# Scaling seven float64 weight pieces on GpSimd, with a new order table, in an attention and expert kernel

## The chip, the cores and the metric

The kernel runs on one core of a Trainium2 chip. The metric is the device time of one execution in microseconds (us); lower is better. The core's engines each follow a queue of their own: TensorE (PE; its weight loads are listed apart as PEld), VectorE (DVE), ScalarE (ACT), GpSimd (POOL) and SyncE (SP), which issues nearly all transfers.

## The reference

Three stages follow one another on 4 batches of 576 tokens: Nyström attention with 32 landmarks and a six-step inverse, a gated layer with 512 inputs and 1536 hidden columns, and eight routed experts.

```python
A = sm(q, k_lm);  Bm = sm(q_lm, k_lm);  C = sm(q_lm, k)
Z = Bm.transpose(0, 1, 3, 2) / (norm1(Bm) * norminf(Bm) + 1e-06)
for _ in range(6):
    Z = 2 * Z - Z @ Bm @ Z
x = A @ Z @ C @ v

xn = x / np.sqrt(np.mean(x * x, axis=-1, keepdims=True) + 1e-06) * rms_g
g = xn @ w_gate
x = (g * (1.0 / (1.0 + np.exp(-g))) * (xn @ w_val)) @ w_out

# routed experts: tokens with x @ w_skip > 0 pick the expert e of the largest logit
out = x + gate_w * (np.maximum(x @ w1[e], 0.0) @ w2[e])   # other tokens: out = x
```

The change concerns w_gate and w_val, each 512x1536. They reach the kernel, as w_out does, as **float64**, while the engines compute in 32 bits.

## The kernel before, in words

**Stages.** `attention()` computes one batch; the first batch's attention takes the first 55 us or so. The gated layer then runs as eight units (`run_unit`, lines 1302 to 1336), each of half a batch (288 tokens). A unit goes over 12 columns of 128 hidden features: products pg (gate) and pv (value), the activation in `hidden_g` and `hidden_v`, and the result split into a high and a low 32-bit-rounded part, h_t. Then the "o" products with w_out follow. The later batches' attention runs beside the first units. The routed experts (products ph and py) come last.

**Attention is multiplied into the weights.** The layer's input is attention's A (normalised, ap, split into ap_t) times a small matrix WT per head pair; so the kernel first multiplies WT into the weights, P = WT x w, and splits P into two parts (a ScalarE cast and a VectorE subtraction). For one batch P is made in column groups q = 0 to 2 (tiles P_678, P_682, P_1001). The factor 1/rms reaches ap by way of sq, ms, a square root on ScalarE (rbs), a reciprocal on VectorE, the rb products and the copies of rb to rbs.

**From float64 to 32 bits.** w_gate and w_val come in 12 pieces (`PARTS`, line 917; for each q two of w_gate and two of w_val), each one load of 1 MB into one of three raw buffers (`load_raw`, tiles wr). `from_f64` (lines 826 to 846) makes a piece in four steps:

1. *scaling*: the upper word of each number, read as a 32-bit float, times a power of two, into a tile s (two buffers);
2. a conversion on ScalarE of the top 16 bits to integers (wo<-wr, int32<-uint16);
3. a conversion on ScalarE that writes the half word (wo<-wr, f16<-f32);
4. *joining* on VectorE: shift s by three bits and OR it in (SCALAR_TENSOR_TENSOR wo<-s,wo).

`convert_w(i)` (line 870) calls it with the engines `EARLY` for pieces 0 to 4 and `LATE` for 5 to 11 (the seven later pieces). The load of piece i+3 needs the raw buffer of piece i, so steps 1 to 3 of piece i must be over. The finished piece is also written to a spill in memory (wg_d, wv_d), from which later batches read it. `convert_wout` does the same for the 12 pieces of w_out (wf<-wo, x<-wo on ScalarE, then a split, whose subtraction alternates between VectorE and GpSimd).

**The order.** `ORDER` (lines 38 and on) holds for TensorE, VectorE, ScalarE, GpSimd and SyncE a list of signed numbers, pairs of a jump and a run length. `arrange()` walks each list and chains the engine's instructions in the order that it gives. So each engine's order is written out by hand, instruction by instruction. An engine executes its queue in that order, and a step that waits holds all that stand behind it.

Line numbers are those of the kernel before (those of after are larger by 13). Most of the profile's rows carry L175 or L198, the lines of the helper through which all instructions are recorded, so tile names tell the rows apart.

Of the kernel before, what the change touches and what calls it, by code (L numbers as in the profile page):

```python
# [11 lines left out]
ALU = mybir.AluOpType  # L12
# [19 lines left out]
F64_BIAS = 2.0**-112  # L32
# [7 lines left out]
    for s in (  # L40
# [162 lines left out]
def attention_moe_kernel(  # L203
# [644 lines left out]
    EARLY, LATE, WOUT = (V, A, A), (V, A, A), (V, A, A)  # L848
# [689 lines left out]
```

## Time and profile before

| | |
|---|---|
| median of three runs | 656.9 us (655.61 to 657.79) |
| profiled execution | 652.86 us |
| its span, first to last instruction | 651.1 us |
| mean granted TensorE clock | 0.975 |
| TensorE busy | 615.8 us, 95% |
| VectorE busy | 435.4 us, 67% |
| ScalarE busy | 271.0 us, 42% |
| GpSimd busy | 142.6 us, 22% |

All views come from one profiled execution. The granted clock is a share of full speed: 1.00 is 2.4 GHz and 0.50 is 1.2 GHz. Busy times of single stages tell more than those of the span, as the stages have different limits.

### The profile page before, as it was taken

Reading aid. Unit: us, or ns where it says so; the run is one execution under the profiler, and the core shown is the slowest. Engines: PE = TensorE matmul, PEld = TensorE weight load, DVE = VectorE, ACT = ScalarE, POOL = GpSimd, SP = SyncE. Lnnn points to the kernel's source line nnn. Section 1 sums busy time; section 2 is a strip of 40 time slices with the busy share of each in tenths; the row PEclk is TensorE's granted clock in tenths of the full one; section 3 lists DMA queues with packets and bytes.
Section 4 is the critical chain, followed back from the end, with each engine's and each line's share of the span. In section 5 each row is a group of like instructions: output and inputs, shape, how many; then the busy total and the mean of one; then the engine's idle time right before and its main releaser. Section 6 shows DMA issues by size and latency. Waiting matters only on the chain.

```text
span 651.1 us, 12738 instructions
## 1 busy us (share of the span) xinstructions
PE 615.8 (95%) x4712; PEld 536.8 (82%) x4712; DVE 435.4 (67%) x1013; ACT 271.0 (42%) x583; POOL 142.6 (22%) x162
## 2 busy tenths in 40 slices
PE   5878689999989999999999999999999999999996
PEld 5755469888858889779988878999998989989985
DVE  8888878989778788879589773723626344354361
ACT  2676779342155224435323443412533434333240
POOL 5000234322004104201401310321632133033030
PEclk9868789999999999999999999999999999999999
DMA  9887990541365222169122043302175476183363
GB/s 293 286 259 272 373 403 5 174 118 49 90 227 199 59 91 74 36 231 266 42 74 56 2 146 111 114 2 81 56 205 154 147 232 190 47 256 105 111 210 122
DMA packets 68685, 97.13 MB, mean 149 GB/s; under 512 B 11152, under 2 KB 46224, under 8 KB 68624
## 3 DMA queue, kind: packets, MB, share of 16 engines
q1 hardware_dynamic: 68624, 96.33, 46.1%
q8 instruction: 37, 0.61, 0.4%
q14 instruction: 24, 0.20, 0.1%
HBM read 76.97 MB, written 19.34 MB: 148 GB/s over the span
## 4 chain that ended last, share of the span: by engine, by line
PE 58%; DMA 2%; DVE 1%; POOL 1%; ACT 1%; issue 0%; ACTq 0%; DVEq 0%; POOLq 0%
PE o L175 12%; PE py L175 12%; PE ph L175 12%; PE pv L175 8%; PE pg L175 7%; PE P L175 2%; PE sq L175 1%; DMA w1r<-in_moe_w_dram 1%; PE nr L175 1%; PE lp L175 1%; DMA w2r<-in_moe_w_dram 1%; PE sk L175 1%; POOL xsl L175 1%; PE cT L175 0%; PE rb L175 0%
## 5 line engine op out<-in xcount | busy, mean ns | idle before, releaser
L175 PE MATMUL o<-h_t,wo 128*128 128x288 f32 x1152 | 164.0, 298 | 0.8 <-DVE wo L175 0.7
L175 PEld LDWEIGHTS o<-h_t,wo 128*128 128x128 f32 x1152 | 154.5, 188 | 10.4 <-issue 8.1
L175 POOL TENSOR_TENSOR h_t<-h,h_t 128x288 fp32r<-128x288 f32 x96 | 80.8, 845 | 323.7 <-ACT h_t L175 279.1
L175 PE MATMUL pv<-ap_t,P 128*128 128x288 f32 x576 | 100.7, 308 | 6.4 <-ACT P L175 4.4
L175 PE MATMUL pg<-ap_t,P 128*128 128x288 f32 x576 | 100.1, 307 | 4.5 <-ACT P L175 2.4
L175 PEld LDWEIGHTS pg<-ap_t,P 128*128 128x128 f32 x576 | 85.1, 194 | 13.0 <-ACT P L175 5.1
L175 PEld LDWEIGHTS pv<-ap_t,P 128*128 128x128 f32 x576 | 85.3, 195 | 11.5 <-ACT P L175 7.4
L175 PE MATMUL ph<-xsh,P 128*128 128x288 f32 x384 | 77.6, 297 | 0.0
L175 ACT ACTIVATE h<-pg 128x288 f32<-128x288 f32 x96 | 39.4, 411 | 66.9 <-PE pg L175 63.3
L175 PEld LDWEIGHTS ph<-xsh,P 128*128 128x128 f32 x384 | 61.7, 188 | 0.6
L175 DVE SCALAR_TENSOR_TENSOR h<-h,pg 128x288 f32<-128x288 f32 x96 | 43.0, 448 | 27.3 <-ACT h L175 27.2
L175 PE MATMUL ph<-xsl,P 128*128 128x288 f32 x192 | 55.5, 296 | 0.0
L175 PE MATMUL py<-wo,h_t 128*128 128x512 f32 x210 | 52.2, 395 | 0.0
L175 ACT CAST h_t<-h 128x288 fp32r<-128x288 f32 x96 | 40.8, 430 | 24.6 <-DVE h L175 24.3
L175 DVE TENSOR_TENSOR h<-h,pv 128x288 f32<-128x288 f32 x96 | 43.0, 451 | 9.6 <-PE pv L175 3.3
L175 PEld LDWEIGHTS py<-wo,h_t 128*128 128x128 f32 x210 | 39.3, 188 | 9.5
L175 POOL TENSOR_TENSOR P<-w1r,P 128x512 fp32r<-128x512 f32 x16 | 21.0, 1311 | 83.6 <-ACT P L175 81.5
L175 DVE STREAM_TRANSPOSE T<-kq 64x576 f32<-64x576 f32 (+1 forms) x40 | 35.6, 891 | 5.2 <-DMA kq<-in_q_dram 4.2
L175 DVE SCALAR_TENSOR_TENSOR h_t<-ph,h_t 128x288 fp32r<-128x288 f32 (+2 forms) x45 | 14.5, 353 | 32.4 <-ACT h_t L175 32.4
L175 PEld LDWEIGHTS ph<-xsl,P 128*128 128x128 f32 x192 | 35.7, 188 | 0.2
L175 DVE TENSOR_TENSOR P<-P,P 128x512 fp32r<-128x512 f32 x48 | 31.2, 682 | 4.9 <-ACT P L175 4.7
L175 ACT CAST P<-w1r 128x512 fp32r<-128x512 f32 x32 | 19.9, 621 | 32.5 <-DMA w1r<-in_moe_w_dram 31.6
(215 smaller groups left out, 830.0 us busy)
## 6 DMA issues: line engine op xcount, KB each, us to landing
wl<-wg_d SPq DMA_DIRECT2D x18, 512.0 KB, 5.1
wr<-wv_d SPq DMA_DIRECT2D x16, 512.0 KB, 4.8
w1r<-in_moe_w_dram SPq DMA_DIRECT2D x32, 256.0 KB, 3.1
wr<-in_moe_w_gate_dram SPq DMA_DIRECT2D x6, 1024.0 KB, 8.4
wr<-in_moe_w_val_dram SPq DMA_DIRECT2D x6, 1024.0 KB, 6.2
wo<-in_moe_w_out_dram SPq DMA_DIRECT2D x12, 512.0 KB, 10.0
wo<-in_moe_w_dram SPq DMA_DIRECT2D x24, 256.0 KB, 5.2
kq<-in_k_dram SPq DMA_DIRECT2D x8, 576.0 KB, 4.6
```

Of the source, the lines that this page charges most:

```text
L175: ins = f(*args, **kw)
```

## The change

`from_f64` lets its scaling run on the engine that it is given, not always on VectorE, and `LATE` names GpSimd for it. All five lists of `ORDER` are new. Every instruction other than the seven scalings stays on its engine.

```diff
@@ the table: all five lists are replaced; the first line of the first list @@
-        "0 9 2 9 -11 2 9 5 3 4 -7 3 4 5 2 17 -18 1 -2 1 18 9 1 1 -2 1 5 1 -4 1 -2 1 1 2 1 "
+        "0 9 2 9 -11 2 9 16 3 17 -20 2 25 3 -28 1 17 7 3 2 3 1 -4 3 1 1 1 1 -2 1 1 5 5 1 "
...
@@ -832,7 +845,7 @@
         if on[0] is A:
             A.activation(s, hi, AF.Copy, scale=F64_BIAS)
         else:
-            V.tensor_scalar(s, hi, F64_BIAS, None, ALU.mult)
+            on[0].tensor_scalar(s, hi, F64_BIAS, None, ALU.mult)
         if on[1] is A:
             A.activation(di, top, AF.Copy, scale=LOW_BITS)
         else:
@@ -845,7 +858,7 @@
             di, si, 3, di, ALU.logical_shift_left, ALU.bitwise_or
         )
 
-    EARLY, LATE, WOUT = (V, A, A), (V, A, A), (V, A, A)
+    EARLY, LATE, WOUT = (V, A, A), (G, A, A), (V, A, A)
     wsrc = {"g": w_gate, "v": w_val}
     wparts = {}
 
```

In the rows below, wr is a raw piece, s_822 to s_988 are the scaled tiles of the seven later pieces, and wo the converted piece. GpSimd, from the end of the landmark sums (ln) on, before:

```order
L175 TENSOR_TENSOR ln<-s_340 128x64
L175 TENSOR_TENSOR h_t<-h,h_t 128x288 x7
L175 TENSOR_TENSOR wo<-wf,wo 128x512
L175 TENSOR_TENSOR h_t<-h,h_t 128x288 x2
L175 TENSOR_TENSOR wo<-x_1184,wo 128x512
```

and after:

```order
L188 TENSOR_TENSOR ln<-s_340 128x64
L188 TENSOR_SCALAR s_822<-wr 128x1024
L188 TENSOR_SCALAR s_831<-wr 128x1024
L188 TENSOR_SCALAR s_840<-wr 128x1024
L188 TENSOR_SCALAR s_883<-wr 128x1024
L188 TENSOR_SCALAR s_942<-wr 128x1024
L188 TENSOR_SCALAR s_981<-wr 128x1024
L188 TENSOR_TENSOR h_t<-h,h_t 128x288
L188 TENSOR_SCALAR s_988<-wr 128x1024
L188 TENSOR_TENSOR h_t<-h,h_t 128x288 x3
L188 TENSOR_TENSOR wo<-wf,wo 128x512
```

Six scalings stand ahead of the first h_t of the layer and one behind it.

VectorE, from the squares (sq) of the first batch's attention to the first h, before:

```order
L175 TENSOR_TENSOR sq<-sq 128x576
L175 TENSOR_SCALAR s_822<-wr 128x1024
L175 TENSOR_SCALAR rbs<-ms 128x144
L175 TENSOR_TENSOR WT<-pw,gcol 128x256
L175 SCALAR_TENSOR_TENSOR wo<-s_822,wo 128x1024
L175 RECIPROCAL rbs<-rbs 128x144
L175 TENSOR_SCALAR s_831<-wr 128x1024
L175 SCALAR_TENSOR_TENSOR wo<-s_409,wo 128x1024
L175 TENSOR_TENSOR ap<-AT,rbs 128x288 x2
L175 TENSOR_TENSOR ap_t<-ap,ap_t 128x288 x2
L175 TENSOR_SCALAR s_840<-wr 128x1024
L175 TENSOR_TENSOR P_678<-P,P_678 128x512 x4
```

and after:

```order
L188 TENSOR_TENSOR sq<-sq 128x576
L188 TENSOR_SCALAR rbs<-ms 128x144
L188 SCALAR_TENSOR_TENSOR wo<-s_822,wo 128x1024
L188 RECIPROCAL rbs<-rbs 128x144
L188 SCALAR_TENSOR_TENSOR wo<-s_831,wo 128x1024
L188 TENSOR_TENSOR ap<-AT,rbs 128x288 x2
L188 TENSOR_TENSOR ap_t<-ap,ap_t 128x288 x2
L188 TENSOR_TENSOR ap<-AT,rbs 128x288
L188 TENSOR_TENSOR P_678<-P,P_678 128x512 x4
L188 SCALAR_TENSOR_TENSOR wo<-s_840,wo 128x1024
L188 SCALAR_TENSOR_TENSOR wo<-s_883,wo 128x1024
L188 SCALAR_TENSOR_TENSOR h<-h,pg 128x288
```

The scalings are gone, WT and the joining of the fifth piece (s_409) have moved up ahead of the squares, a third ap stands ahead of the subtractions of P_678, and two joinings (s_840, s_883) stand between these and the first h.

ScalarE, from the end of the first batch's attention to the first tanh (h<-pg), before:

```order
L175 COPY GT<-pw 128x256
L175 ACTIVATE wo<-wr 128x1024 x4
L175 ACT_TABLE_LOAD
L175 ACTIVATE rbs<-rbs,eps 128x144
L175 COPY rbs<-rb 128x288 x2
L175 CAST ap_t<-ap 128x288 x2
L175 CAST P_678<-P 128x512 x4
L175 ACTIVATE wo<-wr 128x1024
L175 ACT_TABLE_LOAD
L175 ACTIVATE h<-pg 128x288
```

and after:

```order
L188 COPY GT<-pw 128x256
L188 ACTIVATE wo<-wr 128x1024 x5
L188 ACT_TABLE_LOAD
L188 ACTIVATE rbs<-rbs,eps 128x144
L188 ACTIVATE wo<-wr 128x1024
L188 COPY rbs<-rb 128x288 x2
L188 ACTIVATE wo<-wr 128x1024
L188 CAST ap_t<-ap 128x288 x2
L188 CAST P_678<-P 128x512 x4
L188 CAST ap_t<-ap 128x288
L188 ACTIVATE wo<-wr 128x1024
L188 ACT_TABLE_LOAD
```

Of the 24 conversion steps (wo<-wr) of the 12 pieces, 14 stood ahead of the square root's table load before and 16 do after; 14 and 18 ahead of the casts of P_678. The two behind rbs<-rbs,eps belong to the ninth piece (wo_882).

## Rows read from the trace of the kernel before

**Rows 1.** The page: busy time, share of the span, instructions.

```profile
PE 615.8 (95%) x4712; PEld 536.8 (82%) x4712; DVE 435.4 (67%) x1013; ACT 271.0 (42%) x583; POOL 142.6 (22%) x162
```

**Rows 2.** Busy time by stage; the first row names the columns.

```profile
core 0: us, PE busy (x) PEld busy (x) DVE busy (x) ACT busy (x) POOL busy (x), PEclk, DMA share, GB/s
56.58:98.46 41.88, 33.24 (x208) 26.48 (x209) 33.91 (x60) 33.29 (x58) 11.05 (x11) 0.80 0.92 352
98.46:119.64 21.18, 20.39 (x147) 19.36 (x146) 18.82 (x27) 16.27 (x28) 9.45 (x8) 1.00 0.17 53
119.64:645.00 525.36, 519.62 (x4060) 460.06 (x4061) 332.66 (x767) 190.77 (x445) 113.54 (x118) 1.00 0.40 124
```

**Rows 3.** Groups in 56.58 to 98.46: count, busy us, mean ns, idle before.

```profile
L175 PE MATMUL pg<-ap_t,P 128*128 128x288 f32 x72 | 15.9, 357 | 3.7 <-ACT P L175 2.4 <-DVE P L175 1.3
L175 PE MATMUL pv<-ap_t,P 128*128 128x288 f32 x72 | 15.1, 358 | 6.2 <-ACT P L175 4.4 <-DVE h L175 1.7
L175 PE MATMUL P<-wo,WT 64*32 64x512 f32 x64 | 6.0, 596 | 0.0
...
L175 ACT ACTIVATE wo<-wr 128x1024 int32<-128x1024 uint16 (+1 forms) x10 | 12.4, 1270 | 2.8 <-DMA wr<-in_moe_w_val_dram 2.8
L175 ACT ACTIVATE wf<-wo 128x512 int32<-128x512 uint16 (+1 forms) x7 | 4.9, 724 | 0.4 <-DVE wo L175 0.2
```

**Rows 4.** The page, costliest groups: the "o" products.

```profile
L175 PE MATMUL o<-h_t,wo 128*128 128x288 f32 x1152 | 164.0, 298 | 0.8 <-DVE wo L175 0.7
```

**Rows 5.** Timeline: start us, us, instruction [idle before <- releaser].

```profile
73.95 1.12 ACT L175 ACTIVATE wo<-wr 128x1024 int32<-128x1024 uint16 x1 [2.76 <-DMA wr<-in_moe_w_val_dram]
...
76.26 0.85 PE L175 MATMUL pv<-ap_t,P 128*128 128x288 f32 x2 [4.44 <-ACT P L175]
```

**Rows 6.** Busy time of the two stretches around that wait.

```profile
71.64:76.26 4.62, 0.18 (x1) 0.00 (x1) 2.35 (x6) 2.31 (x5) 1.81 (x3) 0.55 1.03 417
76.26:82.30 6.04, 6.04 (x24) 5.78 (x24) 6.04 (x10) 4.49 (x7) 0.33 (x1) 0.50 1.02 417
```

**Rows 7.** Tile s: scalings and joinings, ns minimum, median, maximum, starts.

```profile
L175 DVE TENSOR_SCALAR s<-wr x12: 628/685/687, 13.3 to 78.4; 128x1024 f32<-128x1024 f32 x12
L175 DVE SCALAR_TENSOR_TENSOR wo<-s,wo x12: 1205/1217/1221, 17.5 to 80.1; 128x1024 int32<-128x1024 int32 x12
```

**Rows 8.** Timeline: a scaling. Then SyncE's waits for scalings, 20 to 90 us.

```profile
48.70 0.69 DVE L175 TENSOR_SCALAR s<-wr 128x1024 f32<-128x1024 f32 x1
...
SPq L198 <- DVE s L175: 21.7, 8, 5.3
```

**Rows 9.** Groups of the whole span on GpSimd.

```profile
L175 POOL TENSOR_TENSOR wo<-wo 128x512 fp32r<-128x512 f32 x8 | 11.0, 1390 | 17.9 <-ACT wo L175 12.6 <-DMA wo<-in_moe_w_dram 5.2
...
L175 POOL TENSOR_TENSOR sT<-sT,arec 128x576 f32<-128x576 f32 x4 | 4.7, 1170 | 29.6 <-DVE bdk L175 19.0 <-DVE arec L175 7.8 <-PE pb L175 2.8
```

**Rows 10.** Timeline: a joining on VectorE, and h_t on GpSimd twice.

```profile
64.94 1.22 DVE L175 SCALAR_TENSOR_TENSOR wo<-s,wo 128x1024 int32<-128x1024 int32 x1
65.07 1.75 POOL L175 TENSOR_TENSOR h_t<-h,h_t 128x288 fp32r<-128x288 f32 x1 [51.88 <-ACT h_t L175]
...
75.80 0.79 POOL L175 TENSOR_TENSOR h_t<-h,h_t 128x288 fp32r<-128x288 f32 x1 [2.81 <-ACT h_t L175]
```

**Rows 11.** Timeline: ScalarE ahead of the first pg, and that pg.

```profile
45.40 2.52 ACT L175 ACTIVATE wo<-wr 128x1024 int32<-128x1024 uint16 x2 [0.89 <-DMA wr<-in_moe_w_val_dram]
...
53.51 0.70 ACT L175 COPY rbs<-rb 128x288 f32<-128x288 f32 x2 [3.31 <-PE rb L175]
...
55.95 2.04 ACT L175 CAST P<-P 128x512 fp32r<-128x512 f32 x4
...
56.58 0.53 PE L175 MATMUL pg<-ap_t,P 128*128 128x288 f32 x2 [1.25 <-ACT P L175]
```

**Rows 12.** Tile wr, issue to landing: loads issued in 39 to 45; at 49.5.

```profile
DMA to landing us min/median/max: 5.0/5.6/6.2
...
DMA to landing us min/median/max: 7.8/7.8/7.8
```

243 rows, old and new, of the table ORDER are left out of this document.

## The prediction, made before the changed kernel was timed

> **What bounds the kernel now.** I read the page's busy times first, then busy time by stage, and only then who waits for whom.
>
> TensorE is busy 95% of the span, no other engine over 67% [rows 1]. A share of that height hides where time can be won. So the stages matter [rows 2]. From 119.64 us to 645 us TensorE is busy 519.62 of 525.36 us at the full granted clock: 5.7 us of idle in four fifths of the kernel. In 98.46 to 119.64 us, the "o" products, it is busy 20.39 of 21.18. What is left is the first 98.46 us, and of those 56.58 to 98.46 is the stretch in which the first gated layer starts while its weights are still being turned from float64 to float32. There TensorE is busy 33.24 of 41.88 us at a granted clock of 0.80, with ScalarE busy 33.29, VectorE 33.91 and the DMA engines at 0.92 of their time.
>
> How much is there to win? TensorE executes 144 pg and pv matmuls there and 64 of P [rows 3]. The "o" matmuls, of the same 128x288 shape, take 164.0/1152 = 0.142 us each when nothing is late [rows 4]. So the stretch needs 144 x 0.142 + 6.0 = 26.4 us and takes 41.9. At most 15.5 us can come back, and an edit gets only the part whose wait it removes.
>
> Which wait ends last? TensorE's waits in the stretch are 4.4 + 2.4 us for ScalarE's casts of P, 1.7 for VectorE's h and 1.3 for VectorE's P, in the last column of the same rows. The 4.4 us one is a chain that can be read step by step: ScalarE stands 2.76 us for a weight load (w_val) until 73.95, executes a conversion step of 1.12 us, and only then casts the P that pv needs at 76.26 [rows 5]. The loss goes on after it: the clock was granted at 0.55 while TensorE stood (71.64 to 76.26) and at 0.50 in the next 6.04 us, in which 24 matmuls filled all the time (0.25 us each against 0.142) [rows 6]. That is 24 x (0.25 - 0.142) = 2.6 us more. So ScalarE's queue in this stretch is the limit, with VectorE right behind it. I make the sum on ScalarE's queue.
>
> **The change part by part.** The profiled execution took 652.86 us (span 651.1, 1.8 around it); the median of the three timed runs is 656.9, 4.0 above. I work out a difference and apply it to both.
>
> *Seven scalings leave VectorE.* A scaling took 0.685 us, so 7 x 0.685 = 4.8 us leave VectorE [rows 7]. Those seven began between 48.70 and 78.4 us. The one for the sixth piece started at 48.70 although nothing but VectorE's order held it: the loads of raw weights behind such scalings waited 21.7 us in eight waits on SyncE's queue [rows 8]. GpSimd has nothing to do there: its h_t at 65.07 ended 51.88 us of idleness [rows 10].
>
> *What a scaling costs on GpSimd* is not in the trace. From below, VectorE's own 0.685 us. From above, GpSimd's two-input operation of 512 columns at 1.390 us: 2.8 us for 1024. Between them, sT with 576 columns took 1.170 us, and 1.170 x 1024/576 = 2.1 [rows 9]. I take 2.1, since sT's rows are plain 32-bit ones, the nearest shape; a one-input form can be cheaper. The cover: the joining step also needs ScalarE's two conversion steps of the same piece, 2 x 1.27 = 2.5 us from the landing [rows 3]. GpSimd's 2.1 hides behind these if it starts at the landing; at 2.8 it would be 0.3 late for each piece. What may take the cover away is that only two scaled tiles exist, so a third scaling waits for a joining step of VectorE (1.217 us [rows 7]), and that GpSimd and VectorE hinder each other. The trace shows this: h_t took 1.75 us at 65.07 beside a joining step from 64.94 to 66.16, and 0.79 at 75.80 [rows 10]. Price on the path: +0.7 us (one third of one scaling), from 0 to 2.1 (a whole one).
>
> The Trainium skill explains that row (SBUF — State Buffer, "Who interferes with whom"): a VectorE instruction with two SBUF inputs and a GpSimd instruction that reads SBUF lock each other out for a whole instruction, while one-input VectorE instructions outside the fast modes do not. The trace agrees with 1.75 against 0.79 us. The skill also speaks against the change (GPSIMD Engine Reference, "Performance versus the Vector engine"): elementwise work is about twice as slow on GpSimd. An estimate by that page is 2 x 0.685 = 1.4 us for a scaling; the sum would keep its cover.
>
> *ScalarE's order, ahead of the first pg.* Before the square-root table the old order has 14 conversion steps (seven pieces), the new one 16; between there and the casts of P_678 it adds two more, both of the ninth piece (wo_882), one ahead of the rbs copies and one behind them. Old: last step ends at 47.9, table, rbs copies 53.51, casts of P 55.95 to 57.99, first pg 56.58 [rows 11]. New: the load of that ninth piece needs the sixth piece's raw buffer. Its scaling is now early, but ScalarE's second step on it stands behind its first step on the seventh piece. The seventh piece's load (issued 40.4, landed 45.4) moves up by some 2 us with the scaling ahead of it, to about 43.5; two steps of 1.27 later the ninth load is issued, at about 46. Such a load took 7.8 us to land [rows 12], so 53.8. Then: step to 55.0, rbs copies to 55.7, step to 56.9, casts of ap_t to 57.8, casts of P 57.8 to 59.9. Against 57.99 that is +1.9 us. Ends: 0 if the load lands by 52 and VectorE's shorter queue brings rbs forward; +2.9 if the load comes a microsecond later.
>
> *ScalarE's order, from the casts of P_678 to the "o" products.* Four of the ten conversion steps that stood here (12.4 us) have been done already: -4 x 1.27 = -5.1. The 2.76 us wait for the last load goes: that load is issued earlier by the shorter waits on SyncE, and its last steps no longer stand ahead of the ap_t and P_682 casts. In exchange four more conversion steps of w_out come ahead of the twelfth tanh (15, where there were 11): +4 x 0.72 = +2.9 [rows 3]. Together -5.1 - 2.8 + 2.9 = -5.0. The next late thing is then VectorE's h and P (1.7 + 1.3 us).
>
> *The "o" products.* They wait 0.8 us in all for converted w_out [rows 4], and ScalarE reaches these four steps earlier: 0.
>
> *The rest of the table.* Everything later is ordered anew too, with the same instructions. Only 5.7 us of idle are there to win, and another order can lose as well: I take -0.4, from -3 to +2.
>
> Sum: +1.9 - 5.0 + 0.7 + 0 - 0.4 = **-2.8 us**: 650.1 for a profiled execution, **654.1 us** as a median.
>
> **The rivals.**
>
> *Both losses come back.* If ScalarE never runs dry, the 4.4 us stop and the 2.6 us of slow clock behind it both go, and the front costs nothing because VectorE's queue is shorter there: -4.4 - 2.6 + 0.7 = -6.3, 650.6. For: the stop and the slow clock are one chain. Against: VectorE is busy 33.91 of 41.88 us.
>
> *Given back.* ScalarE's gain is real, but half of it only uncovers VectorE's h and P, so -2.5; with +1.9 at the front and +0.7 for GpSimd that is 0.1 us: 657.0. For: VectorE is as busy as ScalarE, and TensorE already waits 3.0 us for it.
>
> *VectorE becomes the bound (slower).* GpSimd's seven scalings are 7 x 2.1 = 14.7 us of reading within about 37 us, a share of 0.4. VectorE has some 13 two-input instructions there (joining steps, ap, ap_t); if 0.4 of them run into a scaling and wait half of one, 13 x 0.4 x 1.05 = 5.5 us, more than the 4.8 that left. Then ScalarE's -5.0 brings nothing, while the front costs its upper 2.9 and GpSimd's chain 0.7: +3.6, 660.5. It decides from the point where VectorE is held for longer than 4.8 us and the ninth piece lands after some 54 us. For: two orders of VectorE's joining steps stand directly ahead of the first h. Against: this kernel's h_t operations on GpSimd collide in the same way and cost TensorE little.
>
> **How the numbers follow.** A measurement of this kernel can tell about 0.3%, 2.0 us, from no change. Forecast 0.36 (its own range 652 to 656.5, nearly all of it over 0.3% faster), both losses back 0.15, given back 0.23, VectorE bound 0.26. Faster: 0.33 + 0.15 = 0.48. Within 0.3%: 0.03 + 0.23 = 0.26. Slower: 0.26. The range reaches from 650.0, just below the best case, to 660.0, which leaves out the worse half of the slower case: the later part's bounds (-3 to +2) spread each case by more than it differs from its neighbour.
>
> **What would show it.** Right: scalings on GpSimd of about 2.1 us that start within a microsecond of their landing; first pg at 58 to 59 us; no wait of ScalarE over 1 us for a w_val load behind the first tanh; no stretch with the clock at 0.50 between the first h and the "o" products; "o" starting near 96; 119.64 to the end as long as before within 2 us. Wrong: GpSimd scalings of 3 us or more, VectorE's joining steps well over 1.217 us, or "o" starting at 98 or later. If "o" starts near 96 and the time has not changed, it was lost in the later part of the table.

## The result

The changed kernel took **646.14 us** (median of four runs, 644.92 to 647.41), the kernel before beside it 656.25: a ratio of 0.9868, with a 95% interval from 0.9829 to 0.9907. That is 10.1 us faster (6 to 11 by the interval), well under the predicted 654.1 and under the lower end of the range, 650.0. The profiled execution took 645.70 us, 7.2 us less than that of before.

The page of after, busy time by engine, to be read beside [rows 1]:

```profile
PE 610.3 (95%) x4712; PEld 534.4 (83%) x4712; DVE 428.1 (66%) x1006; ACT 271.4 (42%) x583; POOL 163.7 (25%) x169
```

VectorE has lost 7.3 us and seven instructions, GpSimd has gained 21.1 us with the same seven. TensorE, which the prediction called full behind 119.64 us, is *busy* for 5.5 us less, with the same 4712 instructions.

Busy time by stage of after, with the columns of [rows 2]:

```profile
56.58:98.46 41.88, 34.15 (x224) 24.22 (x217) 34.38 (x60) 35.99 (x66) 23.87 (x16) 0.90 0.88 334
98.46:119.64 21.18, 21.18 (x162) 21.18 (x161) 18.95 (x33) 14.37 (x27) 8.13 (x6) 1.00 0.25 79
119.64:636.83 517.19, 514.08 (x4044) 458.02 (x4043) 328.70 (x762) 190.29 (x442) 114.70 (x118) 1.00 0.41 125
```

The stretch ahead of 98.46 us does hardly more work than before (224 matmul records against 208); the next 21.18 us do 162 instead of 147, without a gap; and TensorE's work, which went on to 645.7 us before, is over at 636.8 (the last row of [rows 2] stops at 645.0, just ahead of that end).

The scaled tiles of after (tile s, as in [rows 7]):

```profile
L188 DVE SCALAR_TENSOR_TENSOR wo<-s,wo x12: 1162/1216/1324, 19.7 to 78.1; 128x1024 int32<-128x1024 int32 x12
L188 POOL TENSOR_SCALAR s<-wr x7: 2812/2843/3869, 43.6 to 73.0; 128x1024 f32<-128x1024 f32 x7
```

Its timeline ahead of the first pg (as in [rows 11]):

```profile
56.98 1.14 ACT L188 ACTIVATE wo<-wr 128x1024 int32<-128x1024 uint16 x1 [3.57 <-DMA wr<-in_moe_w_gate_dram]
58.00 0.70 ACT L188 COPY rbs<-rb 128x288 f32<-128x288 f32 x2
...
61.13 0.54 PE L188 MATMUL pg<-ap_t,P 128*128 128x288 f32 x2 [1.85 <-ACT P L188]
```

A scaling on GpSimd takes 2.843 us. ScalarE stands 3.57 us for the ninth piece's load ahead of the copies of rb, and in this profile the first pg comes at 61.13 us, not 56.58. Both starts move by some us from one profile to the next, as the experiments show.

### The profile page after: what moved, and what is told of

It reads as the page before. It is cut to its first block, busy times and chain, and to the rows that moved or that the text cites. A ratio compares the mean times of both kernels' runs of the same rounds, so it can differ in the third digit from the quotient of the medians.

```text
span 643.9 us, 12734 instructions
## 1 busy us (share of the span) xinstructions
PE 610.3 (95%) x4712; PEld 534.4 (83%) x4712; DVE 428.1 (66%) x1006; ACT 271.4 (42%) x583; POOL 163.7 (25%) x169
## 4 chain that ended last, share of the span: by engine, by line
PE 79%; DMA 7%; DVE 5%; ACT 4%; issue 2%; SPq 1%; POOL 1%; POOLq 0%; ACTq 0%; DVEq 0%
PE o L188 23%; PE py L188 12%; PE ph L188 12%; PE pv L188 10%; PE pg L188 10%; DMA wr<-in_moe_w_gate_dram 4%; PE P L188 3%; DMA wr<-in_moe_w_val_dram 2%; PE sq L188 2%; PE nr L188 2%; ACT wo L188 2%; PE sk L188 1%; PE lp L188 1%; DMA wr<-wv_d 1%; DVE T L188 1%
## 5 line engine op out<-in xcount | busy, mean ns | idle before, releaser
L188 PEld LDWEIGHTS o<-h_t,wo 128*128 128x128 f32 x1152 | 154.9, 188 | 6.3 <-issue 4.3
L188 PE MATMUL pv<-ap_t,P 128*128 128x288 f32 x576 | 97.3, 302 | 4.1 <-ACT P L188 2.3
L188 PE MATMUL pg<-ap_t,P 128*128 128x288 f32 x576 | 97.5, 304 | 2.8 <-ACT P L188 1.9
L188 PEld LDWEIGHTS pg<-ap_t,P 128*128 128x128 f32 x576 | 83.4, 192 | 10.9 <-DVE h L188 4.3
L188 PEld LDWEIGHTS pv<-ap_t,P 128*128 128x128 f32 x576 | 83.0, 190 | 9.4 <-ACT P L188 2.7
L188 ACT ACTIVATE wo<-wr 128x1024 int32<-128x1024 uint16 (+1 forms) x24 | 29.5, 1257 | 18.9 <-DMA wr<-in_moe_w_gate_dram 16.4
L188 PE MATMUL py<-wo,P 128*128 128x512 f32 x126 | 32.2, 396 | 0.0
```

What stands on the lines that cost most here:

```text
L188: ins = f(*args, **kw)
```

## The experiments

Four theories were open. **A**: the new table makes the time, in two places, and the move of the scalings brings nothing; its rival **B**: the move makes it. **C**: all comes from the first stretch. **D**: the late first pg is a loss on the path; its rival **E**: it is not.

This table gives what TensorE's rows show in each profiled kernel: the start of the first and of the last "o" product, and of the last py product with P (us), and the time against before where it was measured more than once (elsewhere the one time in us). Single profiles of one program differ by some 2 us at these points (the last section gives one reason), so a difference counts here when it exceeds that, when its wait is seen, or when it returns in several profiles. r_after and r_after_v are repeats of after and of k2_after_v.

| kernel | first o | last o | last py | time / before (95% interval) |
|---|---|---|---|---|
| before | 98.5 | 486.1 | 641.8 | |
| after | 98.0 | 478.6 | 632.9 | 0.9868 (0.9829 to 0.9907) |
| k1_before_g | 100.4 | 488.8 | 643.7 | 1.0015 (0.9986 to 1.0044) |
| k2_after_v | 97.6 | 478.8 | 633.0 | 0.9809 (0.9761 to 0.9858) |
| k3_after_early | 97.0 | 482.3 | 638.2 | 0.9933 (0.9900 to 0.9967) |
| k4_before_early | 99.5 | 481.1 | 636.3 | 0.9923 (0.9897 to 0.9949) |
| k5_after_steps_behind | 100.8 | 482.4 | 637.2 | 0.9939 (0.9908 to 0.9971) |
| k6_before_x2t | 99.5 | 487.5 | 643.4 | (655.64) |
| k7_before_step_behind | 96.1 | 484.4 | 641.1 | 1.0004 (0.9969 to 1.0039) |
| k8_after_v_steps_behind | 100.1 | 479.4 | 633.8 | 0.9903 (0.9872 to 0.9934) |
| k9_after_to_98 | 97.8 | 488.0 | 643.8 | (655.41) |
| r_after | 97.3 | 476.5 | 631.0 | 0.9843 (0.9805 to 0.9881) |
| r_after_v | 97.8 | 478.4 | 632.7 | 0.9804 (0.9762 to 0.9845) |
| k11_after_v_step_ahead | 97.0 | 477.6 | 632.1 | 0.9812 (0.9770 to 0.9854) |
| k12_before_to_478 | 97.8 | 485.6 | 642.9 | (655.14) |
| k13_before_to_440 | 99.0 | 488.7 | 643.1 | (655.23) |
| k14_before_to_300 | 99.0 | 487.3 | 641.7 | (654.10) |

### The move without the table, and the table without the move

In the first kernel the order is that of before, and each later scaling has only changed its queue:

```diff
-DVE  TENSOR_SCALAR s<-wr 128x1024      (seven times)
+POOL TENSOR_SCALAR s<-wr 128x1024      (at the same places in time, among h_t)
```

> The order of before on all engines, with one difference: the seven later scalings leave VectorE's queue and stand in GpSimd's, each at the place among the h_t operations at which VectorE had started it. Theory A (the new table makes the time, the move of the scalings alone brings nothing): 0.3 to 3 us slower than before, since a scaling on GpSimd took 2.84 us in the profile of after against 0.685 on VectorE, and here nothing is arranged around that; the joinings wait for them, and the first pg comes later than 56.58 us. Theory B (the move makes the time, because 4.8 us leave VectorE): 2 to 5 us faster than before.

Measured: 654.95 us against 654.51, a ratio of 1.0015. Theory B falls: at best 0.9 us is gained. In the one profile all of TensorE's work stands 1.9 to 2.7 us later than in that of before, within the price that theory A gave; but k6 and k12, which keep before's order up to the last "o", differ there by 1.9 us from each other, and the times give 0.4 us (-0.9 to +2.9), so a price is not shown.

The second is the order of after, with the scalings on VectorE again:

```diff
-            on[0].tensor_scalar(s, hi, F64_BIAS, None, ALU.mult)
+            if on[0] is G:
+                late_s.append(V.eng.tensor_scalar(s, hi, F64_BIAS, None, ALU.mult).ins)
...
-POOL TENSOR_SCALAR s<-wr 128x1024      (seven times)
+DVE  TENSOR_SCALAR s<-wr 128x1024      (behind the joining that frees the tile)
```

> The order of after on all engines, with the seven scalings back on VectorE, each right behind the joining that frees its buffer. Theory A (the table makes the time): within 2 us of after, on either side; the pieces are scaled 2.1 us sooner each, so that the weight loads of the ninth and later pieces may even be issued earlier. Theory B (the move makes the time): 3 to 5 us slower than after, since VectorE gets its 4.8 us back in the stretch in which it is as busy as ScalarE.

> The kernel after once more, beside the next two on one chip. Both theories: 645 to 647 us, 1.2 to 1.5% under before.

> Once more the order of after with the seven scalings on VectorE. Theory A (the place of the scalings brings nothing in this table): within 2 us of the kernel after on the same chip, rather faster than slower. Rival (642.99 was the first sign that the move costs time even here): 2 to 4 us faster than the kernel after, in both runs of this kernel.

Measured: 642.99 us, a ratio of 0.9809; and beside after on one chip 643.39 against 645.56 (0.9804, from 0.9762 to 0.9845, against 0.9843, from 0.9805 to 0.9881). So the table alone gives the whole gain, and the move of the scalings brings nothing: that part of theory A holds. Whether the move costs something is open. Both comparisons put it on the wrong side, by 3.2 us (after and k2 were not timed side by side) and by 2.2; that is the rival's range of the repeat, 2 to 4 us, and just past theory A's 2, but the two intervals overlap.

### The two halves of the table

Each of the next two kernels follows one order up to 119.5 us of its profile (what had started by then) and the other order for the rest. No instruction is added or removed.

```diff
-order of before, all of it
+k3: after up to 119.5 us, then before        k4: before up to 119.5 us, then after
```

> The first 119.5 us in the order of after (scalings on GpSimd), all that after had not begun by then in the order of before. Theory A (the gain has two sources, about 3 us ahead of 119.5 us and the rest spread over the later part, where TensorE was already called full): 2 to 4 us faster than before, and the o products of the first unit end near 119 us as in after. Theory C (all comes from the first stretch, and what the later part shows is only the shift): 6 to 8 us faster than before, as after.

> The mirror: the first 119.5 us in the order of before (scalings on VectorE), all that before had not begun by then in the order of after. Theory A (two sources): 3 to 6 us faster than before, and no sign of it ahead of 119.5 us. Theory C (all from the first stretch): within 1.5 us of before.

Measured: 649.62 us (-4.9) and 649.29 us (-5.2) against 654.51. Theory C falls. Theory A had 2 to 4 us for the first half, too little, and 3 to 6 for the second: the halves are worth about 5 us each and add up to the 10 of the change. In the profile k3's lead of 3.7 us at the last "o" product is 3.6 at the last py, so the lead of the first stretch is kept over the experts.

### The front: what two steps of ScalarE are good for

```diff
 ACT ACTIVATE rbs<-rbs,eps 128x144
-ACT ACTIVATE wo<-wr 128x1024            (ninth piece)
 ACT COPY rbs<-rb 128x288 x2
-ACT ACTIVATE wo<-wr 128x1024            (ninth piece)
 ACT CAST ap_t<-ap 128x288 x2
 ACT CAST P_678<-P 128x512 x4
+ACT ACTIVATE wo<-wr 128x1024 x2         (ninth piece)
```

> The kernel after, with ScalarE's two conversion steps of the ninth piece moved from around the copies of rb to behind the four casts of P_678. Theory D (the front is on the path, as the prediction's sum had it): the copies of rb no longer wait for that piece's load, the first pg comes 3 to 4 us earlier than its 61.13 us, and the o products start 2 to 4 us earlier. Theory E (what the front loses is waited for anyway further on, for later weight loads): the first pg comes earlier as said, but the o products start within 1 us of 97.97, and the time is within 1.5 us of after.

> Both at once: the order of after with the seven scalings on VectorE, and the two steps of the ninth piece behind the casts of P_678. Theory D: 2 to 4 us faster than the kernel with the scalings on VectorE alone (642.99). Theory E: within 1.5 us of it, 641.5 to 644.5.

Measured: 649.76 us, a ratio of 0.9939 against 0.9868, which is *slower* than after by 3.6 us in the medians and 4.6 in the ratios; with the scalings on VectorE 646.44 (0.9903 against 0.9809), slower than without the edit by 3.5 and 6.2 us. Theory D falls, and E as well, since the first "o" moves to 100.8 us. The first pg comes at 58.48 us, but this says little: after, its repeat, k3 and k9, which all follow after's order up to here, have it at 61.13, 57.83, 56.46 and 61.64 us, and their first "o" at 98.0, 97.3, 97.0 and 97.8. Here are ScalarE and TensorE further on, in the timeline of k5:

```profile
69.70 3.58 ACT L190 ACTIVATE wo<-wr 128x1024 int32<-128x1024 uint16 x3 [2.88 <-DMA wr<-in_moe_w_val_dram]
...
73.45 1.07 ACT L190 CAST P<-P 128x512 fp32r<-128x512 f32 x2
...
74.82 2.54 PE L190 MATMUL P<-wo,WT 64*32 64x512 f32 x12 [4.32 <-DVE P L190]
```

and the same places in the timeline of after:

```profile
68.25 3.69 ACT L188 ACTIVATE wo<-wr 128x1024 int32<-128x1024 uint16 x3 [0.32 <-DMA wr<-in_moe_w_val_dram]
...
73.46 1.67 PE L188 MATMUL P<-wo,WT 64*32 64x512 f32 x12 [0.83 <-DVE P L188]
```

The twelfth and last load needs the raw buffer of the ninth piece, so it needs these two steps. SyncE issues it at 62.48 us in the timeline of k5:

```profile
62.48 0.37 SPq L213 DMA_DIRECT2D wr<-in_moe_w_val_dram  x1
```

and in the timeline of after:

```profile
60.08 0.37 SPq L211 DMA_DIRECT2D wr<-in_moe_w_val_dram  x1
```

It lands later, the casts that stand behind its steps on ScalarE wait with it, and TensorE stops for 4.32 us instead of 0.83. Behind the stop the clock is at its lower level, as in [rows 6] of before:

```profile
70.50:74.82 4.32, 0.00 (x0) 0.00 (x1) 1.97 (x3) 4.32 (x7) 1.18 (x2) 0.98 1.02 416
74.82:78.86 4.04, 4.03 (x17) 1.60 (x17) 3.32 (x6) 4.01 (x9) 3.19 (x2) 0.50 1.02 419
```

(Columns as in [rows 2]: a granted clock of 0.50 from 74.82 on, in k5.) So the early place of the two steps, which the prediction entered as a loss, is what moves the last load up, and the first pg does not set the end of the stretch. In before that load was issued at 65.08 us and waited for until 73.95 [rows 5]:

```profile
65.08 0.37 SPq L198 DMA_DIRECT2D wr<-in_moe_w_val_dram  x1
```

That the last load paces after itself is not shown. In the four profiles named above it is issued at 60.08, 57.45, 56.07 and 60.27 us, and yet their first "o" products start within 1.0 us of each other. k3 has the earliest of them, with a stop of 3.19 us:

```profile
71.08 2.54 PE L179 MATMUL P<-wo,WT 64*32 64x512 f32 x12 [3.19 <-DVE P L179]
```

What paces the stretch once this load is early stays open.

The same edit in the other direction, in the kernel with the scalings on VectorE, where ScalarE stood 2.44 us for rb between the two steps:

```diff
 ACT ACTIVATE wo<-wr 128x1024            (ninth piece)
+ACT ACTIVATE wo<-wr 128x1024            (ninth piece)
 ACT COPY rbs<-rb 128x288 x2
-ACT ACTIVATE wo<-wr 128x1024            (ninth piece)
```

> The order of after with the scalings on VectorE, and ScalarE's second conversion step of the ninth piece right behind its first, ahead of the copies of rb for which ScalarE stood 2.4 us in that kernel. Theory G (the last weight load sets the end of the first stretch; it needs this step, which is why moving both steps back made the o products 2.9 us later): the twelfth load is issued 1 to 1.5 us earlier than 58.8, the o products start 1 to 2 us earlier, the time is 1 to 2 us shorter. Rival (the last load is no longer what is waited for): within 0.7 us at the o products.

Measured: the last load is issued at 56.67 us against 57.93 in the repeat on the same chip, the first "o" starts at 97.0 against 97.8, and the time is 643.65 against 643.39: no gain. Theory G's sizes fail, but for the earlier issue; the 0.8 us at the first "o" is just past the rival's 0.7, and the time is as the rival has it: issued this early, the load need no longer be what is waited for last.

The stop of 4.4 us in before was tried by itself:

```diff
-ACT ACTIVATE wo<-wr 128x1024            (waits 2.76 us for the last load)
 ACT CAST ap_t<-ap 128x288
 ACT CAST h_t<-h 128x288
 ACT CAST P_682<-P 128x512 x2
+ACT ACTIVATE wo<-wr 128x1024
```

> The kernel before, with one ScalarE instruction moved: the conversion step that waited 2.76 us for the last weight load (73.95 us) stands behind the second pair of P_682 casts, not ahead of the ap_t and h_t casts and these. Theory F (that step in that place made TensorE's 4.4 us wait, and this wait with the slow clock behind it was the first stretch's loss): pv at 76.26 comes 1.3 us earlier or more, the o products start 1.5 to 3 us earlier. Rival (the joining of the last pieces, for which this step is now late, is what the rest waits for): the o products start within 0.7 us of before, the wait having moved to the P that needs these pieces.

Measured: TensorE waits 1.89 us at this pv, not 4.44:

```profile
74.61 0.54 PE L177 MATMUL pv<-ap_t,P 128*128 128x288 f32 x2 [1.89 <-ACT P L177]
```

And the first "o" starts at 96.1 us, 2.4 us earlier than in before and 1.7 earlier than in any other profile of before's order (97.8 to 99.5), so theory F holds for the stretch. But the time is 653.93 against 654.20, no gain. The lead is 1.7 us at the last "o" and 0.7 at the last py. Where it goes is the next subject.

### The later half: a wait behind the wait

TensorE's visible wait of before there is 1.4 us at 488 us, lp for ScalarE's copy x2T, which stands behind four casts of expert weights (w2r). In the next kernel that copy alone is moved:

```diff
+ACT ACTIVATE x2T<-o 128x288
 ACT CAST wo<-w2r 128x512 x4
-ACT ACTIVATE x2T<-o 128x288
```

> The kernel before, with one ScalarE instruction moved: the last copy of o products (x2T) stands ahead of the four casts of w2r behind which it waited from about 486 to 489.23 us. Theory A (a part of the gain behind 119.5 us is this one wait of TensorE, 1.4 us at 488): the o products up to 486 us as before, the routed experts' products 1.3 to 1.7 us earlier against them. Rival (the wait is covered by something else, a weight load or VectorE's share of x2T): less than 0.5 us.

Measured: the wait for x2T is gone, and at 510 us another of 1.5 us stands in its place. TensorE's waits (total us, times, longest) from 478 to 560 in before:

```profile
PE lp L175 <- ACT x2T L175: 1.4, 1, 1.4
```

and in k6:

```profile
PE ph L176 <- DVE h_t L176: 1.5, 1, 1.5
```

Against its own last "o" (487.5) the last py comes at +155.9 us, before had +155.7: nothing is left of the gain. In k7 both waits stand there (1.4 and 0.8 us), and the second takes back half of its lead; in k3 they are 0.8 and 0.5 us.

In after both waits are gone; in k4, which follows after's order there, 0.6 us of the second is left. From the last "o" to the last py it takes 154.9 to 156.7 us in the five profiles with before's order (before, k1, k3, k7, k9) and 154.2 to 155.2 in the ten with after's. Where does that come from? Three kernels follow before up to a point and then after:

> The order of before up to 478 us, all that had not begun by then in the order of after. Theory A: as before up to the end of the o products at 486, then 2.4 to 3 us earlier by the first py products, since both waits go, that of lp for x2T (1.4 us) and that of ph for h_t which had come in its place when x2T alone was moved (1.5 us). Rival: one comes for the other again, less than 1 us.

> The order of before up to 440 us, then that of after. Theory I (SyncE's order is the cause at the routed experts: their weight loads are issued some 10 us sooner, so that ScalarE's casts of them are over before x2T and h_t are wanted): as before up to 486 us within 0.7 us, no wait for x2T or h_t, and 2.0 to 3.5 us earlier at the later ph products (545 us on). Rival (it needs the order of the units before too): less than 1 us.

> The order of before up to 300 us, then that of after. If the later part's gain is spread evenly over its units: 2.5 to 4 us earlier than before at 486 us and at 545. If it comes from the unit that follows 119.5 us alone: less than 1.5 us at 486.

With the switch at 478, the expectation failed. TensorE's waits from 478 to 560 in that kernel:

```profile
PE lp L178 <- ACT x2T L178: 1.5, 1, 1.5
PE ph L178 <- DVE h_t L178: 1.0, 1, 1.0
```

Both are there, and from the last "o" to the last py it takes 157.3 us, 1.6 more than before. With the switch at 440, neither is (no wait of TensorE from 440 to 560 is listed), and from the last "o" (488.7, 2.6 us behind before and so outside the 0.7 expected, 1.4 of it for a load, below) to the last py (643.1) it takes 154.4 us, 1.3 less than before: below the 2.0 to 3.5 expected, but as in the profiles with after's order. So what removes the waits lies in the order between 440 and 478 us. There SyncE issues the experts' weight loads (w1r) sooner. The rows of tile w1r give the starts of the first and the last of eight, in before:

```profile
L198 SPq DMA_DIRECT2D w1r<-in_moe_w_dram x8: 372/383/407, 464.3 to 479.2; - x8
```

in after:

```profile
L211 SPq DMA_DIRECT2D w1r<-in_moe_w_dram x8: 373/376/407, 454.4 to 466.8; - x8
```

and in k13, with the switch at 440:

```profile
L201 SPq DMA_DIRECT2D w1r<-in_moe_w_dram x8: 372/376/407, 464.0 to 476.6; - x8
```

In k13 they come 2.9 to 5.2 us sooner against the last "o" than in before. ScalarE's order of the casts in the same stretch is also that of after, so the loads are the likely cause and not the shown one.

With the switch at 300, neither expectation came true: the last "o" is 1.2 us *behind* before, and the last py 0.1 ahead. A longer wait of TensorE near 190 us for a load (below) hides the gain, so the stretches are to be compared by their lengths (us, from the starts of TensorE's "o" and py products; the fifth unit's first "o" starts at 320.4 us in before, 319.4 in k4, 325.5 in k14 and 316.9 in after):

| stretch | before | k4 | k14 | after |
|---|---|---|---|---|
| first "o" to the fifth unit's first "o" | 221.9 | 219.9 | 226.5 | 218.9 |
| fifth unit's first "o" to the last "o" | 165.7 | 161.7 | 161.7 | 161.7 |
| last "o" to the last py with P | 155.7 | 155.2 | 154.4 | 154.3 |

Of the 6.5 us by which k4 is shorter, 3.9 lie from the fifth unit's "o" products to the last, 2.1 ahead of them and 0.5 at the experts. The middle row is hardly touched by noise: it is 165.6 to 165.9 us in all seven profiles with before's order there and 161.7 to 162.0 in all nine with after's. (k14's first number holds the unit in which the orders change, 1.8 us longer than in before, and the late load.) So the gain is neither even nor all in the unit behind 119.5 us: the greatest part comes from the order of the units between 320 and 427 us.

### The "o" products

> The order of after up to 97.9 us (the start of the o products), then that of before. Theory H (the o products gain because more of w_out is converted when they start): they take 20.5 us without a wait for w_out, as in after, and stand 3.5 us or more ahead of before at their end. Rival (the gain is the order inside them, with products of the next unit placed between): TensorE's weight loads wait 1 to 2 us for w_out again, and half of the lead or more is gone at their end.

Measured: the 144 products start at 97.8 and the last at 117.4, 19.6 us, where before has 98.5 to 119.3, 20.8 us; one wait for w_out is left. After has 98.0 to 118.5, but 12 products of the next unit lie between (1.6 us), so 18.9. Neither expectation came true as it was put: the lead at their end is 1.9 us, not 3.5 or more, and the weight loads still wait 0.6 us for w_out. By these lengths about two thirds of the 1.9 us between before and after come from the work ahead of 98 us (theory H), a third from the order inside; this is an estimate from single profiles. Further on this kernel lost its lead: 488.0 at the last "o". 1.4 us of that are a longer wait for the load wr<-wv_d than in before (2.0 against 0.6 us); the rest was not looked into, so k9 says nothing on the later half.

## Why the prediction was wrong

**The end of the first stretch** was forecast rightly as the place, and wrongly in its working. Up to the end of the "o" products the sum was -2.4 us; k3 gives -4.9 (-2.2 to -6.5).

- *Front, +1.9 as a loss on the path.* The first pg is 4.5 us later in this pair of profiles (the ninth load took 8.8 us to land), but it lies at 56.6 to 59.5 us in six profiles with before's order up to there (before, k4, k6, k12, k13, k14) and at 56.5 to 61.6 in the four with after's: 0.8 us in the mean. Above all, it is not on the path: the first "o" starts at 97.0 to 98.0 us in those four, whenever the first pg comes. The step that failed is that the sum followed ScalarE's queue up to the first pg, and did not follow the raw buffers from these two steps to the last load. k5 puts the price of the opposite order at 3.6 to 4.6 us.
- *ScalarE's queue behind the casts, -5.0.* From the first pg to the first "o" it took 41.9 us before and 36.8 after, 5.0 less, but that was luck of the pair: the repeat of after and k3 took 39.5 and 40.5 us, and k12, with before's order, 39.2. What can be told is the sum of front, queue and GpSimd's price, forecast at -2.4: the first "o" starts at 97.8 to 99.5 us in the six profiles with before's order and at 97.0 to 98.0 in the four with after's, 1.4 us earlier in the mean. It did not reach the "96" of the forecast. The slow clock behind a stop [rows 6] is no fixed loss either. The repeat of after, busy times with the columns of [rows 2]:

```profile
75.10:84.00 8.90, 6.34 (x32) 4.82 (x31) 8.43 (x15) 4.64 (x10) 2.50 (x2) 0.50 1.02 416
```

  Its clock was at 0.50 for 8.9 us, and at 0.80 in the mean of 56.58 to 98.46 us, where after has 0.90; yet its first "o" is 0.7 us earlier than after's.
- *GpSimd's price.* A scaling took 2.843 us, at the upper bound of 2.8, where 2.1 was chosen. The path price of 0.7 (0 to 2.1) was low by k2 and its repeat, 3.2 and 2.2 us, but neither they nor k1's runs tell it clearly from zero. The nearest row for 1024 columns was the two-input one of 512 columns (1.390 us), not sT. The Trainium skill (GPSIMD Engine Reference, "Performance versus the Vector engine") has elementwise work about twice as slow there; here it is 2.843/0.685 = 4.2 times, and the measurement decides.
- *The rival in which VectorE becomes the bound* needed 5.5 us of hindrance on VectorE. The joining steps took 1.216 us in the median, as before, with a maximum of 1.324; it was the scaling that was held, up to 3.869 us. In k1 one joining took 2.117. By the rule of the Trainium skill (SBUF — State Buffer, "Who interferes with whom") whoever comes second waits for the whole instruction. The traces agree with it in one direction only. The scaling that started at 65.40 us, beside a joining from 65.20 to 66.45, took 3.869 us, 1.0 more than the others. But a joining that started in the middle of a scaling was not held until its end:

```profile
52.44 2.81 POOL L188 TENSOR_SCALAR s<-wr 128x1024 f32<-128x1024 f32 x1 [1.78 <-DVE wo L188]
54.42 1.16 DVE L188 SCALAR_TENSOR_TENSOR wo<-s,wo 128x1024 int32<-128x1024 int32 x1
```

  It was over 0.33 us behind the scaling's end. Two more such joinings in after took 1.23 and 1.32 us. So in after it was GpSimd that paid, and the measurement decides. The joining of 2.117 us in k1 started 0.06 us behind a scaling of 2.83 and was held for some 0.9.
- *The "o" products, 0.* This is the place where the wrong row was read. [rows 4] gives TensorE's matmuls 0.8 us of idle in all. The row of the weight loads (PEld) of the same 144 products shows what is behind it. Before, from 98.46 to 119.64:

```profile
L175 PEld LDWEIGHTS o<-h_t,wo 128*128 128x128 f32 x144 | 19.3, 188 | 1.8 <-DVE wo L175 1.2 <-POOL wo L175 0.3 <-ACT wo L175 0.3
```

After, from 97.97 to 119.64:

```profile
L188 PEld LDWEIGHTS o<-h_t,wo 128*128 128x128 f32 x144 | 19.2, 188 | 0.0
```

**The rest of the table, -0.4 (-3 to +2)**, is the step that put the time outside the range: it brought 5.2 us (k4, 3.3 to 6.7). The argument was that TensorE has only 5.7 us of idle there. But an "o" matmul's record lasts 0.298 us while one takes 0.142 [rows 4], so a wait of up to 0.15 us behind a matmul shows as no idle at all, and switches between kinds of matmul are many. The ceiling was to be read from PEld. From the first "o" to the last py with P, columns as in [rows 2], in before:

```profile
98.46:641.81 543.35, 536.82 (x4193) 476.83 (x4191) 351.48 (x794) 207.04 (x473) 122.99 (x126) 1.00 0.39 121
```

in k4, with before's first stretch and after's later part:

```profile
99.53:636.34 536.81, 533.45 (x4192) 477.02 (x4191) 351.12 (x794) 207.54 (x473) 123.97 (x126) 1.00 0.40 123
```

The weight loads are busy for the same time, and the stretch is 6.5 us shorter. PEld's idle falls by all of that (543.35 - 476.83 = 66.5 us to 59.8), PE's by about half (6.5 to 3.4). Two units, from the fifth unit's first "o" to the seventh's, show it most sharply, in before:

```profile
320.38:426.80 106.42, 106.21 (x929) 91.48 (x927) 74.97 (x181) 39.61 (x99) 19.85 (x24) 1.00 0.24 77
```

and in k14, with after's order there:

```profile
325.55:428.15 102.60, 102.01 (x914) 90.19 (x913) 74.19 (x176) 36.97 (x92) 19.56 (x25) 1.00 0.24 75
```

That is 3.8 us where before shows 0.2 us of idle on PE; 1.3 of them are 14 weight loads that stand in other units there, 2.5 are idle of PEld. PEld's 66.5 us are no forecast, only a ceiling that does not hide the gain. Two groups of the whole span show the same as shorter *busy* time of the same instructions, before:

```profile
L175 PE MATMUL P<-wl,WT 64*32 64x512 f32 x160 | 15.1, 598 | 0.0
...
L175 PE MATMUL P<-wr,WT 64*32 64x512 f32 x128 | 9.9, 599 | 1.1 <-DMA wr<-wv_d 0.6 <-ACT rbs L175 0.5
```

and after:

```profile
L188 PE MATMUL P<-wl,WT 64*32 64x512 f32 x160 | 14.1, 599 | 0.1
...
L188 PE MATMUL P<-wr,WT 64*32 64x512 f32 x128 | 8.8, 596 | 1.2 <-DMA wr<-wv_d 1.2
```

The P products for the later batches take 2.1 us less, at about the same mean of one: they overlap more in the new order. Which moves of instructions do it was not tried one by one, so that cause stays open.

**The chances.** "Faster" had 0.48. The two rivals that gave the gain back rested on VectorE as the next limit, and on the loss at the front; neither was there. The nearest case, both losses back (0.15), still ended at 650.6, since it too left the later part at nothing. Of the signs, "119.64 to the end as long as before within 2 us" failed most plainly: from the first "o" to the last py it took 534.9 us after and 543.4 before.

## What to carry to other kernels

Before calling an engine full, read the idle time of its weight loads too: where two matmuls' records overlap, as here, the busy time hides every wait that is shorter than the overlap. When a step moves ahead on a queue, follow what it *frees* (here a raw buffer, and through it the last load), not only whom it delays. And take away a wait alone before counting on it: of the two tried so, one came back at once as another (k6), and the other's gain was mostly gone by the end (k7).

## What the runs showed of the hardware

Profiles of one program differ by a single transfer. The load wr<-wv_d, read back from the spill near 190 us, was waited for between 0 us (the repeat of after has no such row) and 2.3 us. TensorE's waits from 140 to 220 us in the kernel with the switch at 300:

```profile
PE P L183 <- DMA wr<-wv_d: 2.3, 1, 2.3
```

The kernel before has 0.6 there, k13, which follows the same order up to 440 us, 2.0, and after 1.2. Nothing of this comes from the change, and it is larger than several of the effects studied here.
